# Cluster attention and a softplus layer on one core: the first pass's scores laid upright, a softplus of three operations, loads on SyncE, and the last outputs in other banks

## The chip, the core and the metric

The kernel runs on one core of a Trainium2 chip. TensorE (PE) multiplies matrices into PSUM, VectorE (DVE), ScalarE (ACT) and GpSimd (POOL) work on tiles, and SyncE (SP) issues transfers; DMA engines carry them. The engines run beside each other, each through its own list of instructions in a fixed order, and wait for each other by semaphores. The metric is the time of one execution in microseconds (us) on the device. Before the change the median of three runs is 899.57 us (896.24 to 903.73).

## The reference

```python
# q, k, v: 4 batches x 8 heads x 768 x 64;  centroids: 8 heads x 16 x 64
q_assign = argmax(q_n @ c_n.T); k_assign = argmax(k_n @ c_n.T)   # normed rows, per head
scores = where(q_assign == k_assign, (q @ k.T) / 8, -1e9)
scores -= max(scores);  attn = exp(scores);  attn /= sum(attn) + 1e-9
x = (attn @ v), heads side by side                               # 3072 x 512
h = x @ w_in                                                     # 512 x 2048
g = maximum(h, 0) + log1p(exp(-abs(h)))                          # softplus
out = g @ w_out                                                  # 3072 x 512
```

All inputs are of 32 bits, except the weights, which arrive as 64-bit floats and are converted on the chip. A query attends to the keys of its own cluster alone.

## The kernel before

**Splitting.** Products are made of 16-bit halves: a value is a high half and a low remainder, and three products stand for one. A head's q rows, and its k rows, become two blocks of 128 rows each for the score product: one holds high and low halves of the 64 features, the other the high half again with 16 columns for the cluster (names `n1`, `n2`, turned into `qt` and `kt`). In `kt` the cluster columns hold minus a large number where the key is in another cluster, so the product itself does the masking.

**Tiles and passes.** There are eight passes `pi`, two for each batch, of three blocks of 128 queries; a pass runs over 8 heads, so it has 24 tiles, 192 in all. For a tile, `scores` makes the 128 x 768 product with four matmuls (L576) in a bank pair of the PSUM pool `ps_s` (two of them), DVE takes the row maximum (L592), ACT the exponential (L600). From the second pass on, ACT and POOL split the result in halves (L639, L641) and a DMA transpose, a *flip*, on SP turns two tiles at a time (`pt<-phl`, L226). In the first pass the 32-bit result is turned on PE instead: six transposes (L617) whose results are copied out by ACT (L625) and DVE (L623); the row sums come from the exponential. `attend` multiplies with V: L679 in 32 bits in the first pass, L683 to L685 later. After two heads `attend` divides by the sums (L702, L703, L710: `x`), splits, and flips the result into `xT`.

**The layers.** `ffn1` makes a block of 128 of the 2048 hidden features for 384 queries (L752 to L754), `softplus` has five operations for it (L771, L773, L774, L783 and, for two blocks, L794 and L795), and `ffn2` (L817 to L819) sums eight blocks in the one bank of `ps_o`, which `store` empties on DVE (L833, L837) before the next block of queries may use it. `prep_weights` converts the weights in 32 steps: ACT, DVE three times (L322, L326, L332), ACT, POOL (L336). `prep_k`, `prep_q` and `prep_v` load and lay out the inputs; those of the first pass are turned on PE, the later ones by flips.

**What sets the order.** The whole program is written as generators that yield operations with an engine and a cost in ns. The class `Order` runs them through a small model of the engines and emits each instruction when the model would start it: of all operations that are ready it takes the one that can start first, then the one with the smaller due number. Each engine's list is the result. Where the model sees PE idle for over 600 ns it puts in `int(gap * 0.65 / 52)` small matmuls, *fillers* (L204). Loads of inputs and weights are issued by ACT (L221), flips and stores by SP. A changed cost or operation so moves instructions on every engine.

Of the kernel before, what the change touches and what calls it, by code (L numbers as in the profile page):

```python
# [25 lines left out]
NPE = 8  # L26

# [86 lines left out]
def tile_cluster_attention__then__softplus_ffn(  # L114
# [47 lines left out]
    cf = cpool.tile([P, D], F32, name="cf")  # L162
    nc.sync.dma_start(cf, centroids.rearrange("h c d -> (h c) d"))
    tab = cpool.tile([P, 2 * NT, NCL], F16, name="tab")
# [9 lines left out]
    eye32 = p2.tile([P, P], F32, tag="ot", name="eye32", bufs=QT)  # L174
    nc.gpsimd.tensor_copy(eye32, eye)
# [10 lines left out]
    for i in range(2):  # L186
        t = cpool.tile([P, 2 * NT, P], F16, name=f"n2_{i}")
        nc.gpsimd.memset(t[:, :, D + NCL :], 0.0)
        N2.append(t)


    od = Order()

    eye32_key = od.get("ot", QT)[1]
# [25 lines left out]
    def load(dst, src, nbytes):  # L220
        return op("ACT", 60, lambda: nc.scalar.dma_start(dst, src), dma=nbytes / 290.0)  # L221
# [10 lines left out]
    def prep_centroids():  # L232
        sq = p2.tile([P, D], F32, tag="x32", name="csq", bufs=1)
# [124 lines left out]
    def prep_v(n: int):  # L358

        vk = yield from ring("vb", NP)  # L360
        rk, vf = yield from raw_tile("v", n, [P, 2, NT, D])
        yield load(vf, rows(v, n, 0, NT, 2), P * 2 * NT * D * 4)
        vb = VB[n // 2 % NP]
        raw_v[n] = vf, rk
# [39 lines left out]
    def nearest(xs, heads, low: int, sfx: str, twin: int):  # L404
# [28 lines left out]
        yield op("DVE", 345, lambda: nc.vector.tensor_tensor(sim, sim, tab[:, :nt], ALU.mult))  # L433
# [50 lines left out]
    def clusters(n, ps, eq, hk):  # L484
# [4 lines left out]
        if h % 4 == 0:  # L489
            alive[n] = p2.tile([P, 4, NCL], F16, tag="al", name=f"al_{n}", bufs=4)  # L490
# [8 lines left out]
    def prep_q(n: int, pi: int):  # L499
# [31 lines left out]
        yield op("DVE", 345, lambda: nc.vector.tensor_scalar(n2[:, :, D : D + NCL], sim, MASK, None, ALU.mult))  # L531

# [8 lines left out]
        )  # L541
        aq = p2.tile([P, c12, 1], F16, tag="aq", name=f"aq_{sfx}")
# [16 lines left out]
    pair, sums = {}, {}  # L559

    def scores(t: int):
# [5 lines left out]
        if t:  # L567
            yield wait("sc", t - 1)
# [4 lines left out]
        def emit():  # L573
            for s in range(2):
                for j in range(2):
                    nc.tensor.matmul(  # L576
                        st[:, j, :SH],
                        qt[:, s, i],
                        kt[:, s, NT // 2 * j : NT // 2 * (j + 1)],
# [15 lines left out]
        tot = {}  # L595
        if pi == 0:
            if n // 2 not in sums:
                sums[n // 2] = p2.tile([P, 2 * QT, 1], F32, tag="sum", name=f"sum_{n}", bufs=NP)
            tot["accum_out"] = sums[n // 2][:, n % 2 * QT + i]
        yield op("ACT", 900, lambda: nc.scalar.activation(p32, st[:, :, :SH], AF.Exp, bias=negm, **tot))  # L600
        od.set(sk)
        if pi == 0:

# [23 lines left out]
            if t == H * QT - 1:  # L627
                od.set(eye32_key)
# [286 lines left out]
```

## Time and profile before

| | |
|---|---|
| median of 3 runs | 899.57 us |
| profiled execution, span of its instructions | 899.4 us; no other time is given for it |
| granted clock of PE, mean | 0.992 |
| PE busy | 859.1 us (96%) |
| DVE, ACT, POOL busy | 576.5, 588.2, 528.1 us |
| queue of SP (flips, stores) | 99.15 MB, 56.2% of the DMA engines' span |
| queue of ACT (loads) | 35.66 MB, 13.4% |

A row of the groups reads: line, engine, operation, out<-in by the program's names, shapes and count, then busy us, mean ns of one, and the idle time of the engine just before with what ended it. The chain of waits follows back from the last instruction to what released it. In the table by stages each stretch has the busy time of each engine with its count, PE's granted clock, the mean share of the DMA engines in use and GB/s. Busy times of PE are of matmuls with their latency, so a stream of 512-column matmuls 0.22 us apart shows 0.38 us for each.

### The profile page before, as it was taken

To read this page: it belongs to the slowest core of one execution; us is meant where nothing else is said; L and a number is where in the kernel's file an instruction comes from. 1 tells how busy PE (TensorE), PEld (TensorE's weight loads), DVE (VectorE), ACT (ScalarE), POOL (GpSimd) and SP (SyncE) were. 2 spreads that over 40 slices of the span, in tenths; PEclk is the share of its full clock that TensorE was granted. 3 is DMA by queue.
4 is the path that set the end of the run, shared out by engine and by line. 5 is a ranking of instruction groups with operands and counts; after the bars stand their busy time and mean duration, and the time that the engine had idled before them with its cause. 6 is when DMAs were issued, how large, how long until landed. Compare 5 with 4: busy or idle time off the path is not lost.

```text
span 899.4 us, 20880 instructions
## 1 busy us (share of the span) xinstructions
PE 859.1 (96%) x8650; PEld 562.1 (62%) x8650; DVE 576.5 (64%) x1060; ACT 588.2 (65%) x904; POOL 528.1 (59%) x353
## 2 busy tenths in 40 slices
PE   7889998989889999999999999999999999999997
PEld 7878876655565666655666665555666565655554
DVE  4989997778876656765757666657675655433331
ACT  5667686866757677865858777766787576633330
POOL 5322356787857678866757677675777665512110
PEclk8999999999999999999999999999999999999999
DMA  6323759988896879999696989997888655510000
GB/s 202 117 89 112 154 150 214 202 194 212 168 190 150 189 151 191 226 201 210 149 198 126 187 166 193 195 220 135 182 182 186 145 119 134 111 30 12 25 0 36
DMA packets 393326, 136.12 MB, mean 151 GB/s; under 512 B 369680, under 2 KB 386064, under 8 KB 393232
## 3 DMA queue, kind: packets, MB, share of 16 engines
q1 hardware_dynamic: 371472, 99.15, 56.2%
q10 hardware_dynamic: 21760, 35.66, 13.4%
q8 instruction: 67, 1.10, 0.5%
q14 instruction: 27, 0.22, 0.1%
HBM read 35.68 MB, written 6.29 MB: 47 GB/s over the span
## 4 chain that ended last, share of the span: by engine, by line
PE 73%; DVE 8%; DMA 8%; ACT 4%; issue 3%; POOL 3%; ACTq 1%; POOLq 0%; DVEq 0%
PE s L576 10%; PE o L817 8%; PE o L819 8%; PE o L818 8%; PE h L752 8%; PE h L754 8%; PE h L753 8%; DMA pt<-phl 8%; PE mbank L679 3%; PE mbank L683 3%; PE mbank L685 3%; PE mbank L684 3%; POOL phl L641 2%; PE pT L617 2%; DVE negm L592 2%
## 5 line engine op out<-in xcount | busy, mean ns | idle before, releaser
L641 POOL TENSOR_TENSOR phl<-p,phl 128x768 f16<-128x768 f32 x168 | 278.3, 1672 | 84.8 <-ACT phl L639 61.2
L592 DVE TENSOR_REDUCE negm<-s 128x1 f32<-128x768 f32 x192 | 182.6, 954 | 51.5 <-PE s L576 48.0
L600 ACT ACTIVATE p<-s,negm 128x768 f32<-128x768 f32 x192 | 172.1, 898 | 65.6 <-DVE negm L592 45.5
L795 POOL TENSOR_TENSOR gh<-fg,gh 128x768 f16<-128x768 f32 x64 | 107.2, 1676 | 135.2 <-ACT gh L794 131.8
L752 PE MATMUL h<-xT,wi 128*128 128x384 f16 x512 | 167.4, 327 | 7.4 <-DVE fg L783 5.4
L754 PE MATMUL h<-xT,wi 128*128 128x384 f16 x512 | 167.8, 328 | 0.0
L753 PE MATMUL h<-xT,wi 128*128 128x384 f16 x512 | 167.6, 327 | 0.0
L576 PE MATMUL s<-kt,qt 128*128 128x384 f16 x768 | 155.5, 325 | 3.7 <-ACT p L600 3.3
L819 PE MATMUL o<-wo,gh 128*128 128x512 f16 x384 | 145.8, 380 | 1.1 <-POOL gh L795 1.1
L817 PE MATMUL o<-wo,gh 128*128 128x512 f16 x384 | 146.0, 380 | 0.7 <-DVE ot L837 0.4
L818 PE MATMUL o<-wo,gh 128*128 128x512 f16 x384 | 145.9, 380 | 0.0
L773 ACT ACTIVATE fa<-fa 128x384 f32<-128x384 f32 x128 | 66.6, 521 | 120.1 <-DVE fa L771 119.2
L639 ACT CAST phl<-p 128x768 f16<-128x768 f32 x168 | 134.3, 827 | 16.3 <-DMA pt<-phl 14.1
L771 DVE TENSOR_SCALAR fa<-h 128x384 int32<-128x384 int32 x128 | 71.0, 555 | 107.7 <-PE h L754 107.4
L683 PE MATMUL mbank<-vb,pt 128*128 128x65 f16 x1008 | 108.5, 192 | 8.2 <-DMA pt<-phl 7.8
L684 PE MATMUL mbank<-vb,pt 128*128 128x64 f16 x1008 | 108.5, 192 | 0.0
L685 PE MATMUL mbank<-vb,pt 128*128 128x65 f16 x1008 | 108.2, 194 | 0.0
L683 PEld LDWEIGHTS <-pt 128*128 128x128 f16 x1008 | 93.4, 98 | 22.9 <-DMA pt<-phl 11.4
L783 DVE SCALAR_TENSOR_TENSOR fg<-h,fa 128x384 f32<-128x384 f32 x128 | 70.5, 552 | 53.5 <-ACT fa L774 51.6
L576 PEld LDWEIGHTS <-qt 128*128 128x128 f16 x768 | 71.6, 98 | 49.4 <-issue 6.2
L684 PEld LDWEIGHTS <-pt 128*128 128x128 f16 x1008 | 92.9, 97 | 11.1
L685 PEld LDWEIGHTS <-pt 128*128 128x128 f16 x1008 | 93.1, 97 | 0.0
(122 smaller groups left out, 1289.9 us busy)
## 6 DMA issues: line engine op xcount, KB each, us to landing
wo<-in_moe_w_in_dram ACTq DMA_DIRECT2D x16, 512.0 KB, 3.7
wo<-in_moe_w_out_dram ACTq DMA_DIRECT2D x14, 512.0 KB, 4.0
rawk<-in_k_dram ACTq DMA_DIRECT2D x16, 384.0 KB, 4.7
rawv<-in_v_dram ACTq DMA_DIRECT2D x16, 384.0 KB, 4.6
rawq<-in_q_dram ACTq DMA_DIRECT2D x16, 384.0 KB, 4.1
out_dram<-ot SPq DMA_DIRECT2D x24, 256.0 KB, 2.6
pt<-phl SPq DMA_TRANSPOSE x84, 5.7
wraw<-in_moe_w_out_dram ACTq DMA_DIRECT2D x2, 512.0 KB, 5.3
```

Source lines behind the costliest of these rows:

```text
L576: nc.tensor.matmul(st[:, j, :SH], qt[:, s, i], kt[:, s, NT // 2 * j : NT // 2 * (j + 1)], start=(s == 0), stop=(s == 1),)
L592: yield op("DVE", 950, lambda: nc.vector.tensor_reduce(negm, st[:, :, :SH], AX.XY, ALU.max, negate=True))
L641: "POOL", 1640, lambda: nc.gpsimd.tensor_tensor(phl[:, u, 1], p32, phl[:, u, 0], ALU.subtract), shared=True
L683: nc.tensor.matmul(av, pt[:, 0, c], vb[:, c, D : 2 * D + 1], start=(c == 0), stop=False)
L684: nc.tensor.matmul(av[:, :D], pt[:, 0, c], vb[:, c, :D], start=False, stop=False)
L685: nc.tensor.matmul(av, pt[:, 1, c], vb[:, c, D : 2 * D + 1], start=False, stop=(c == NT - 1))
L752: nc.tensor.matmul(hp, w[0], x[0], start=(c == 0), stop=False)
L753: nc.tensor.matmul(hp, w[0], x[1], start=False, stop=False)
L754: nc.tensor.matmul(hp, w[1], x[0], start=False, stop=(c == NP - 1))
L817: nc.tensor.matmul(po, g[0], wo[:, f, 0, 0], start=(f == f0), stop=False)
L818: nc.tensor.matmul(po, g[0], wo[:, f, 0, 1], start=False, stop=False)
L819: nc.tensor.matmul(po, g[1], wo[:, f, 0, 0], start=False, stop=(f == f0 + NF // 2 - 1))
```

## The change

**First pass.** A new generator `upright` takes the place of scores, exponential and transposes for the 24 tiles of pass 0. It first makes half of the score product (two matmuls, L586: the block with the cluster columns alone), and DVE takes its row maximum (L599). Two small DVE operations (L603, L604) put the negated maximum into two columns of a 128 x 98 tile `mc`, as a multiple of 2048 and a rest; PE turns this (L607) and ACT copies the two rows into rows 96 and 97 of `qt` (L609). The same rows of `kt` hold 2048 and 1. Then the score product is made with keys on the partitions, in twelve matmuls of 128 columns (L619, L620), and the maximum is taken off in the product. ACT's exponential (L638) writes the turned weights at once. The row sums come from a column of ones in V (L730, L752), which is why V of the first heads is laid in rows of 65 and loaded in two parts. Tiles of later passes leave rows 96 and up out of the second block's product.

**Softplus.** exp, ln(1 + .), and then `max(min(a, 20), h)` in place of `|h|`'s sign trick and sum: L771 goes, and the exponential reads PSUM.

**Loads** are issued by SP, and cost the model 450 ns there. **Last outputs:** in the last pass's second half `ffn2` uses the two bank pairs of `ps_s` in place of `ps_o`.

```diff
     def load(dst, src, nbytes):
-        return op("ACT", 60, lambda: nc.scalar.dma_start(dst, src), dma=nbytes / 290.0)
+        return op("SP", 450, lambda: nc.sync.dma_start(dst, src), dma=nbytes / 290.0)
...
+    def upright(t: int):
...
+                nc.tensor.matmul(
+                    st[:, j, :SH], qt[:SHIFT, 1, i], kt[:SHIFT, 1, NT // 2 * j : NT // 2 * (j + 1)],
+                    start=True, stop=True,
+                )
+        yield op("PE", 330, emit)
...
+        yield op("DVE", 950, lambda: nc.vector.tensor_reduce(negm, st[:, :, :SH], AX.XY, ALU.max, negate=True))
+        yield op("DVE", 90, lambda: nc.vector.tensor_scalar(top, negm, 1.0 / by, None, ALU.mult))
+        yield op("DVE", 90, lambda: nc.vector.scalar_tensor_tensor(rest, top, -by, negm, ALU.mult, ALU.add))
...
+        yield op("PE", 60, lambda: nc.tensor.transpose(out=ps[:KROWS], in_=mc, identity=eye))
+        yield op("ACT", 250, lambda: nc.scalar.copy(qt[SHIFT:KROWS, 1, i], ps[SHIFT:KROWS]))
...
+            for c in range(NT):
+                to = up[:, c // (NT // 2), c % (NT // 2) * P : (c % (NT // 2) + 1) * P]
+                nc.tensor.matmul(to, kt[:, 0, c], qt[:, 0, i], start=True, stop=False)
+                nc.tensor.matmul(to, kt[:KROWS, 1, c], qt[:KROWS, 1, i], start=False, stop=True)
+        yield op("PE", 690, emit)
...
+        yield op("ACT", 830, lambda: nc.scalar.activation(dst, up[:, :, :SH], AF.Exp))
...
     def scores(t: int):
...
+        if pi == 0:
+            yield from upright(t)
+            return
...
             for s in range(2):
+                rows = P if s == 0 else SHIFT
                 for j in range(2):
                     nc.tensor.matmul(
                         st[:, j, :SH],
-                        qt[:, s, i],
-                        kt[:, s, NT // 2 * j : NT // 2 * (j + 1)],
+                        qt[:rows, s, i],
+                        kt[:rows, s, NT // 2 * j : NT // 2 * (j + 1)],
...
     def softplus(pi, f, hp, hk):
...
-            lambda: nc.vector.tensor_scalar(a.bitcast(I32), hp.bitcast(I32), -0x80000000, None, ALU.bitwise_or),
-        yield op("ACT", 520, lambda: nc.scalar.activation(a, a, AF.Exp))
+        yield op("ACT", 500, lambda: nc.scalar.activation(a, hp, AF.Exp))
         yield op("ACT", 520, lambda: nc.scalar.activation(a, a, AF.Ln, bias=1.0))
...
-            "DVE", 550, lambda: nc.vector.scalar_tensor_tensor(g[:, f % 2], hp, 0.0, a, ALU.max, ALU.add)
+            "DVE", 550, lambda: nc.vector.scalar_tensor_tensor(g[:, f % 2], a, TOP, hp, ALU.min, ALU.max)
...
     def ffn2(pi: int, half: int, i: int):
...
+        if pi == len(passes) - 1 and half:
+            ok = yield from ring("s", 2)
+            po = ps_s.tile([P, 2, DM], F32, tag="s", name=f"o_{b}_{c0 + i}_{half}")[:, 0]
```

The order on DVE from the first row maximum of the first pass, before (`negm` is the maximum, `ptf` the turned weights of a tile, `wo` and `wi` a weight block under conversion):

```order
L592 TENSOR_REDUCE negm_0_1102<-s_0_1081 128x1
L592 TENSOR_REDUCE negm_1_1107<-s_1_1101 128x1
L332 SCALAR_TENSOR_TENSOR wo<-wo 128x512
L326 SCALAR_TENSOR_TENSOR wo<-wo,wi 128x512
L592 TENSOR_REDUCE negm_2_1143<-s_2_1114 128x1
L623 COPY ptf_0_1115<-pT_0_1_1145 128x384
L592 TENSOR_REDUCE negm_0_1164<-s_0_1148 128x1
L332 SCALAR_TENSOR_TENSOR wo<-wo 128x512
L322 TENSOR_SCALAR wi<-wi 128x512
L623 COPY ptf_0_1115<-pT_1_1_1166 128x384
```

The same engine and place after the change (`mc` is the small tile of the maximum), from the third maximum on:

```order
L599 TENSOR_REDUCE negm_2_1177<-m_2_1136 128x1
L599 TENSOR_REDUCE negm_0_1179<-m_0_1157 128x1
L603 TENSOR_SCALAR mc_118<-negm_2_1177 128x1
L603 TENSOR_SCALAR mc_120<-negm_0_1179 128x1
L604 SCALAR_TENSOR_TENSOR mc_118<-mc_118,negm_2_1177 128x1
L604 SCALAR_TENSOR_TENSOR mc_120<-mc_120,negm_0_1179 128x1
L335 SCALAR_TENSOR_TENSOR wo<-wo,wi 128x512
L599 TENSOR_REDUCE negm_1_1232<-m_1_1181 128x1
L341 SCALAR_TENSOR_TENSOR wo<-wo 128x512
L603 TENSOR_SCALAR mc_118<-negm_1_1232 128x1
L331 TENSOR_SCALAR wi<-wi 128x512
```

The copy of a tile's half is gone and two short operations follow each maximum; weight steps (L331, L335, L341) stand in between more densely: up to the fourth `x` of the program 24 of the 32 blocks are converted, where 18 were.

The order on SP around the first flips of `pt`, before (`xT`, `qt`, `kt`, `pt` are what the flips write):

```order
L226 DMA_TRANSPOSE qt_1_1940<-qn_4_1_1941 128x12x128
L226 DMA_TRANSPOSE pt_4_2031<-phl_3_1980 128x24x128
L226 DMA_TRANSPOSE xT_1420<-xn_0_2056 128x6x128
L226 DMA_TRANSPOSE pt_3_2092<-phl_5_2027 128x24x128
L226 DMA_TRANSPOSE qt_1_1940<-n_1_114 128x12x128
L226 DMA_TRANSPOSE pt_5_2280<-phl_4_2090 128x24x128
```

And after (`wo<-in_moe_w_out` is a weight block's load, `rawq` and `rawk` those of q and k):

```order
L230 DMA wo<-in_moe_w_out_dram 128x512
L230 DMA rawq_2272<-in_q_dram 128x4x192
L235 DMA_TRANSPOSE pt_4_2299<-phl_3_2248 128x24x128
L235 DMA_TRANSPOSE qt_1_2277<-qn_4_1_2278 128x12x128
L235 DMA_TRANSPOSE xT_1524<-xn_0_2313 128x6x128
L230 DMA rawk_2382<-in_k_dram 128x2x384
L235 DMA_TRANSPOSE pt_3_2396<-phl_5_2311 128x24x128
L235 DMA_TRANSPOSE pt_5_2494<-phl_4_2346 128x24x128
L235 DMA_TRANSPOSE kt_2424<-kn_8_2425 128x12x128
L230 DMA wo<-in_moe_w_out_dram 128x512
```

SP's list held flips and stores alone; loads now stand among them, and a load that waits for its buffer stands ahead of flips.

More of the change, by code (lines that the diff above doesn't have):

```diff
@@ L26 @@
 NPE = 8
+TOP = 20.0
+SHIFT = 96
+SHIFT_BY = (2048.0, 1.0)
+KROWS = SHIFT + 2
 REBASE = 2.0**-112
@@ L188, in tile_cluster_attention__then__softplus_ffn @@
         nc.gpsimd.memset(t[:, :, D + NCL :], 0.0)
+        for c, m in zip(range(SHIFT, KROWS), SHIFT_BY):
+            nc.gpsimd.memset(t[:, :, c : c + 1], m)
         N2.append(t)
+    MC = []
+    for i in range(2):
+        t = cpool.tile([P, KROWS], F16, name=f"mc_{i}")
+        nc.gpsimd.memset(t, 0.0)
+        MC.append(t)
     od = Order()
-    eye32_key = od.get("ot", QT)[1]
     mbank = ps_m.tile([P, 512], F32, name="mbank")
@@ L360, in prep_v @@
         vk = yield from ring("vb", NP)
-        rk, vf = yield from raw_tile("v", n, [P, 2, NT, D])
-        yield load(vf, rows(v, n, 0, NT, 2), P * 2 * NT * D * 4)
+        rk, vf1 = yield from raw_tile("v", n, [P, 2, NT, D + (n < H)])
+        vf = vf1[:, :, :, :D]
+        if n < H:
+            yield op("POOL", 150, lambda: nc.gpsimd.memset(vf1[:, :, :, D:], 1.0))
+        parts = 2 if n < H else 1
+        for u in range(0, 2, 2 // parts):
+            yield load(
+                vf[:, u : u + 2 // parts], rows(v, n + u, 0, NT, 2 // parts), P * 2 * NT * D * 4 // parts
+            )
         vb = VB[n // 2 % NP]
-        raw_v[n] = vf, rk
+        raw_v[n] = vf1, rk
         od.set(("vf", n))
@@ L567, in scores @@
         if t:
-            yield wait("sc", t - 1)
+            yield wait("scm" if tiles[t - 1][1] == 0 else "sc", t - 1)
+        if pi == 0:
+            yield from upright(t)
+            return
         sk = yield from ring("s", 2)
@@ L594, in scores @@
         p32 = p2.tile([P, 2, SH], F32, tag="p32", name=f"p32_{sfx}", bufs=3)
[L595 to L600, printed above, removed]
-        od.set(sk)
-        if pi == 0:
-            if u == 0:
-                key = yield from ring("pt", 2)
-                pair[t // 2] = p2.tile([P, 2, NT, P], F32, tag="pt", name=f"ptf_{sfx}"), key
-                od.set(("phl", "new", t))
-            else:
-                yield wait("phl", "new", t - 1)
-            ptf, ptk = pair[t // 2]
-            for j in range(2):
-                hk = yield from ring("h", 2)
-                ps = ps_h.tile([P, NT // 2, P], F32, tag="h", name=f"pT_{sfx}_{j}")
-                def emit(j=j, ps=ps):
-                    for c in range(NT // 2):
-                        nc.tensor.transpose(out=ps[:, c], in_=p32[:, j, c * P : (c + 1) * P], identity=eye32)
-                yield op("PE", 330, emit)
-                dst = ptf[:, u, NT // 2 * j : NT // 2 * (j + 1)]
-                if j:
-                    od.set(pk)
-                    yield op("DVE", 550, lambda: nc.vector.tensor_copy(dst, ps))
-                else:
-                    yield op("ACT", 490, lambda: nc.scalar.copy(dst, ps))
-                od.set(hk)
-            if t == H * QT - 1:
-                od.set(eye32_key)
-            pts[t] = ptf[:, u], ptk
-            od.set(("pt", t))
-            return
+        yield op("ACT", 900, lambda: nc.scalar.activation(p32, st[:, :, :SH], AF.Exp, bias=negm))
+        od.set(sk)
         if u == 0:
```

81 lines of the change are left out of this document (62 added, 19 removed).

## The prediction

> **What bounds the kernel now.** I read the table by stages first, with the borders put at the first score product, the end of the first pass (fourth `x` of L710), the eighth `x`, and the last first-layer matmul. Its columns are the stretch, its length, and the busy time of each engine.
>
> ```profile
> core 0: us, PE busy (x) PEld busy (x) DVE busy (x) ACT busy (x) POOL busy (x), PEclk, DMA share, GB/s
> 0.00:53.10 53.10, 42.73 (x731) 40.70 (x732) 38.48 (x114) 28.73 (x41) 22.75 (x23) 0.94 0.48 156
> 53.10:131.00 77.90, 74.29 (x691) 65.84 (x688) 72.08 (x118) 56.91 (x111) 26.99 (x21) 1.00 0.47 120
> 131.00:245.00 114.00, 100.23 (x1148) 66.97 (x1147) 88.95 (x149) 82.89 (x127) 84.15 (x55) 0.97 0.93 199
> 245.00:300.00 55.00, 50.80 (x585) 34.04 (x583) 38.91 (x71) 37.80 (x56) 34.71 (x24) 1.00 0.85 180
> 300.00:877.30 577.30, 574.07 (x5369) 344.84 (x5366) 334.90 (x606) 379.99 (x569) 357.87 (x231) 1.00 0.72 147
> 877.30:899.40 22.10, 16.95 (x142) 9.69 (x139) 3.19 (x5) 1.88 (x3) 1.64 (x1) 1.00 0.10 36
> ```
>
> From 300 to 877 us PE has work for 574.1 of 577.3 us. Whatever is taken from DVE or ACT there buys at most the 3.2 us left. What can move lies before 300 and in the last 22 us. Part of PE's busy time is filler (L204, matmuls that write nothing anybody reads), as the same table for L204 alone shows; the first number after the length is PE's.
>
> ```profile
> 53.10:131.00 77.90, 7.54 (x126) 7.20 (x126) 1.00 0.47 120
> 131.00:245.00 114.00, 16.18 (x267) 15.12 (x266) 0.97 0.93 199
> ```
>
> So between 131 and 245 us PE has 100.2 − 16.2 = 84.0 us of real work in 114, and no engine is full. Then the chain of waits for these two stages, by line (the views cut these rows off at the right).
>
> ```profile
> by line: PE mbank L679 38.2%; PE pT L617 20.4%; PE s L576 18.4%; PE mbank L204 6.1%; ACT p L600 3.7%; issue 3.5%; DVE negm L592 2.7%; DVE rs L702 2.1%; DVE x L710 1.4%; DVE qn L517 1.2%; DVE ptf L623 0.7%; ACT ptf L625 0.6%; DVE rs L703 0.4
> by line: DMA pt<-phl 10.0%; DVE negm L592 7.4%; PE h L752 7.1%; PE h L754 6.7%; PE h L753 6.6%; issue 5.2%; DVE wo L326 4.7%; PE o L817 4.3%; PE s L576 4.3%; PE o L818 4.1%; PE o L819 4.0%; POOL phl L641 3.9%; PE mbank L683 2.4%; PE mbank L
> ```
>
> In the first pass the chain is PE (77% in three lines), with DVE close behind at 72.1 of 77.9 us busy. In the second stage it changes hands all the time.
>
> **Start (0 to 53).** The loads leave ACT.
>
> ```profile
> 3.75 0.15 DVE L243 TENSOR_SCALAR csg<-css 128x1 f32<-128x1 f32 x1
> ...
> 5.29 1.16 ACTq L221 DMA_DIRECT2D wo<-in_moe_w_in_dram  x1
> 6.50 0.20 ACT L244 ACTIVATE cnrm<-csg 128x1 f32<-128x1 f32 x1 [4.48 <-issue]
> ```
>
> The centroids' logarithm has its input at 3.90 and starts at 6.50, because ACT's sequencer issues loads until 6.45. On SP these stand beside it, and only the centroids' own load goes ahead of the first K load there. All that follows hangs on the centroids, so I take 2.5 us off; the bounds are −4 (later loads come earlier too) and 0 (DVE's work up to 53 us is what counts). The two-part V loads and the small POOL memsets are covered, since nothing reads V before the first scores at 53 us.
>
> **First pass, PE.** Pieces of the chain, with start, length and count:
>
> ```profile
> 38.54 0.37 PE qT L393 x6
> ...
> 58.51 0.65 PE s L576 x4
> 60.44 0.66 PE pT L617 x6
> 65.08 1.29 PE mbank L679 x12
> ```
>
> A tile loses 0.65 + 0.66 = 1.31 us. It gets half a score product (0.33), one small transpose (0.37/6 = 0.06) and twelve 128-column products with their weight loads, for which the six f16 transposes are the nearest row: 2 × 0.37 = 0.74. That is 1.13, or 0.18 less; over 24 tiles **−4.3 us** of PE. The sum column in L730 adds one column to 64: nothing.
>
> **First pass, DVE.** Removed and added, by the rows of the groups (count, busy us, mean ns):
>
> ```profile
> L623 DVE COPY ptf<-pT 128x384 f32<-128x384 f32 x24 | 13.1, 552 | 0.7 <-PE pT L617 0.2
> L702 DVE TENSOR_SCALAR rs<-sum 128x6 f32<-128x6 f32 x4 | 2.4, 602 | 0.0
> L248 DVE SCALAR_TENSOR_TENSOR cnrm<-crn,csg,cnrm 128x1 f32<-128x1 f32 x2 | 1.8, 899 | 0.1
> L249 DVE TENSOR_SCALAR cnrm<-cnrm 128x1 f32<-128x1 f32 x2 | 0.3, 154 | 0.1
> ```
>
> The 24 copies go: −13.1. L752 reads PSUM in place of L702's sums: 2.4 less four at L249's 0.154, so −1.8. For L603 the nearest row is L249: 24 × 0.154 = 3.7. For L604 it is L248, and its two took 0.22 and 1.58 us:
>
> ```profile
> 7.74 1.64 POOL L457 TENSOR_TENSOR kn<-rawk,kn 128x768 f16<-128x768 f32 x1 [5.05 <-ACT kn L455]
> 7.81 1.58 DVE L248 SCALAR_TENSOR_TENSOR cnrm<-crn,csg,cnrm 128x1 f32<-128x1 f32 x1
> ```
>
> The long one ran beside a POOL operation and ended with it. POOL is busy 27.0 of 77.9 us in this stage; with that chance (0.35) of meeting an operation, and half of one to wait (a weight operation of POOL takes 17.11/14 = 1.2 us, next table), L604 costs 0.22 + 0.21, or 10.3 for 24. The ends are 5.3 (none waits) and 37.9 (all do). Sum of the small edits: −13.1 − 1.8 + 3.7 + 10.3 = −0.9, so nothing is won here. The Trainium skill's page "SBUF — State Buffer", section "SBUF: two separate sides", says that a VectorE operation with two SBUF inputs and a GpSimd operation that reads SBUF exclude each other for the whole instruction; L604 is such an operation. By that rule no wait is shared out, and the bad end of 37.9 is reached if POOL always comes first; the pair of rows above agrees.
>
> What DVE does besides matters more. The order shows that up to the fourth `x` it has converted 24 weight blocks (18 before), and up to the first row maximum 5 (4 before). So this stage takes five blocks more, and the next five fewer. Weight work alone, in the table by stages: the second busy time is DVE's, the last POOL's, with one operation for each block (14 and 11).
>
> ```profile
> 53.10:131.00 77.90, 0.00 (x0) 23.38 (x31) 18.00 (x27) 17.11 (x14) 1.00 0.47 120
> 131.00:245.00 114.00, 21.17 (x84) 28.29 (x31) 13.23 (x20) 12.83 (x11) 0.97 0.93 199
> ```
>
> A block costs DVE 23.38/14 = 1.67 us here and 28.29/11 = 2.57 later. DVE's sum is 72.1 − 0.9 + 5 × 1.67 = 79.6 us. At its present filling (72.1/77.9) the stage takes 86.0, **+8.1**; if PE keeps setting the pace, −4.3. Neither row is nearer, so I take the middle, **+2**. ACT loses 24 copies and gains 24 short ones and has 21 us free. PE, DVE and ACT hand a tile on more often now, and its two score products each hold a bank until a reader is done:
>
> ```profile
> L592 DVE TENSOR_REDUCE negm<-s 128x1 f32<-128x768 f32 x192 | 182.6, 954 | 51.5 <-PE s L576 48.0
> L600 ACT ACTIVATE p<-s,negm 128x768 f32<-128x768 f32 x192 | 172.1, 898 | 65.6 <-DVE negm L592 45.5
> ```
>
> That is 0.33 + 0.95 and 0.74 + 0.90 us, 2.9 in all, or 1.5 for each of the two banks, below the 77.9/24 = 3.2 us that a tile takes; so the longer way of a tile is covered by its neighbours.
>
> **Filling stage (131 to 245).** DVE loses five blocks, 5 × 2.57 = 12.9, and one operation of each softplus:
>
> ```profile
> L771 DVE TENSOR_SCALAR fa<-h 128x384 int32<-128x384 int32 x16 | 8.8, 553 | 11.3 <-PE h L754 11.2
> ```
>
> Together 21.7 of its 89.0 us. ACT is rid of its load issues, POOL of five weight operations. The full 21.7 returns if DVE's turns in the chain are what holds the others up; nothing returns if DMA does (share 0.93). DVE holds 7.4% and 4.7% in two lines, DMA 10.0%; I take half, **−11**. After 245 the relief meets a PE at 50.8 of 55, and after 300 a full one: nothing. The order has 31 fillers less than before, 31 × 7.54/126 = 1.9 us of PE, all where PE waits anyway: nothing.
>
> **Tail.**
>
> ```profile
> 877.51 0.56 DVE L771 TENSOR_SCALAR fa<-h 128x384 int32<-128x384 int32 x1 [2.21 <-PE h L754]
> 878.10 0.52 ACT L773 ACTIVATE fa<-fa 128x384 f32<-128x384 f32 x1 [3.46 <-DVE fa L771]
> 882.48 0.39 PE L819 MATMUL o<-wo,gh 128*128 128x512 f16 x1 [1.11 <-POOL gh L795]
> ...
> 882.92 0.38 PE L818 MATMUL o<-wo,gh 128*128 128x512 f16 x1
> 883.14 0.38 PE L819 MATMUL o<-wo,gh 128*128 128x512 f16 x1
> 883.56 0.69 DVE L837 SCALAR_TENSOR_TENSOR ot<-o,ot 128x512 f32<-128x512 f32 x1 [3.79 <-PE o L819]
> 884.30 0.38 PE L817 MATMUL o<-wo,gh 128*128 128x512 f16 x1 [0.20 <-DVE ot L837]
> ```
>
> The last softplus gets from h to ACT 0.59 us sooner, and PE waits for its end at 882.48. Back to back these matmuls start 0.22 us apart, so the bank's drain costs 884.30 − 883.36 = 0.94 us, twice: with scores' banks both go. 0.59 + 1.88 = **−2.5**.
>
> **Sum.** The profiled execution's span is 899.4, 0.2 below the median of the runs shown: 899.4 − 2.5 + 2 − 11 − 2.5 = **885.4**, say 885.5.
>
> **Unpriced: rows of 96 and 98.** No row shows a matmul with fewer than 128 rows.
>
> ```profile
> L576 PEld LDWEIGHTS <-qt 128*128 128x128 f16 x768 | 71.6, 98 | 49.4 <-issue 6.2
> L679 PEld LDWEIGHTS mbank<-rawv,ptf 128*128 128x128 f32 x288 | 34.5, 192 | 0.7
> ```
>
> At 98 ns the load hides under a 0.65/4 = 162 ns product; at the slowest row, 192, each of the 336 shortened products of later passes would show 30 ns, 10 us. I take nothing, as the nearer row is L576.
>
> **Rivals.** *All of DVE's relief arrives*: the first pass keeps PE's pace and the filling stage gives back 21.7: 899.4 − 2.5 − 4.3 − 21.7 − 2.5 = 868.4. For it speaks that no engine's own work is above 0.78 of that stage; against, that every weight block still has to be loaded.
>
> *The filling stage is DMA's*: it returns nothing, and 899.4 − 2.5 + 2 − 2.5 = 896.4 remains, with 892 to 903 around it. For it speaks the share of 0.93: the change moves the transfers to another queue and makes none smaller.
>
> *Slower: SP's queue.* In the order 43 loads stand among the flips after the first `pt` flip, 20 of 84 `pt` flips have one right ahead, and eleven of these loads wait for POOL or ACT to free a buffer. Such a wait holds every flip behind it.
>
> ```profile
> SPq L226 <- POOL phl L641: 123.4, 40, 7.5
> ...
> DMA to landing us min/median/max: 3.2/4.1/9.7
> ```
>
> A wait of SP for POOL lasts 123.4/40 = 3.1 us. Eleven of them, all reaching PE, make 34: 919. The point is (908.6 − 885.5)/3.1 = 7.5 of them. Against it: PE stands still for only 3.2 us in 577 now, so flips have room. The Trainium skill's page "DMA: Bandwidth & Descriptors", section "Queues, rings and completion order", says that a DMA engine takes turns between queues but works through one queue in order. By that rule a load that shares SP's queue, 4.1 us from issue to landing on its own, would also have to outlast the flip in front of it; no row of this case shows a load on SP among flips.
>
> **Chances.** Forecast 0.45, its own range 880 to 892 (the filling stage returns a quarter to three quarters); all relief 0.16; DMA's stage 0.26; SP's queue 0.13. A measurement here tells 1% from no change: 890.6 and 908.6 are the marks. Faster: 0.40 of the forecast's 0.45, and the 0.16, make 0.56. Same: 0.05 + 0.26 = 0.31. Slower: 0.13. The range 868 to 904 leaves out SP's queue and the thin ends of the others.
>
> **What would show it.** The centroids' logarithm near 4 us and the first score product near 50.5. L599 to L604 without 1.6 us operations, or with them. The fourth `x` near 130; if it comes at 124 or 137, the middle was wrong. The eighth `x` at 11 us less after the fourth than the present 114: at the same distance, DMA holds that stage. Between that and the last h PE at 99%; gaps before L734 behind `pt` flips mean SP's queue. No wait for L886 in the last 15 us. A PEld row far above 98 ns for `qt` would make the unpriced term real.

## The result and the profile after

The changed kernel takes 877.05 us in the median of four runs (875.09 to 877.72), beside 900.79 for the kernel before on the same chip (896.24 to 903.73): a ratio of 0.9749, with a 95% interval of 0.9702 to 0.9795. That is 8.5 us below the forecast of 885.5: inside the whole range of 868 to 904, but below the 880 to 892 that the forecast gave as its own. The profiled execution has a span of 873.3 us, 26.1 less than the 899.4 of before.

The table by stages of the changed kernel, with the same borders as in the prediction (first score product, about the fourth and the eighth `x`, last first-layer matmul) and one more at 250. Columns: stretch, length, busy time of each engine, PE's granted clock, DMA share, GB/s.

```profile
core 0: us, PE busy (x) PEld busy (x) DVE busy (x) ACT busy (x) POOL busy (x), PEclk, DMA share, GB/s
0.00:49.70 49.70, 39.73 (x740) 37.78 (x741) 38.67 (x114) 29.62 (x44) 24.27 (x32) 1.00 0.68 209
49.70:130.80 81.10, 75.72 (x901) 68.94 (x899) 72.78 (x156) 53.98 (x95) 31.52 (x26) 1.00 0.41 112
130.80:227.00 96.20, 91.58 (x1061) 62.03 (x1060) 66.97 (x117) 71.57 (x111) 74.84 (x50) 0.98 1.11 218
227.00:250.00 23.00, 22.20 (x258) 15.56 (x257) 18.83 (x31) 17.60 (x26) 15.30 (x11) 1.00 0.82 154
250.00:300.00 50.00, 50.00 (x534) 31.49 (x533) 29.48 (x52) 39.72 (x59) 39.16 (x26) 1.00 1.05 190
300.00:853.60 553.60, 552.76 (x5147) 331.53 (x5145) 274.80 (x485) 361.87 (x548) 339.89 (x220) 1.00 0.80 148
853.60:873.30 19.70, 14.93 (x111) 8.05 (x109) 2.63 (x4) 1.85 (x3) 1.64 (x1) 0.96 0.11 41
```

The same table for the fillers alone (L213 after the change; PE's busy time stands behind the length):

```profile
49.70:130.80 81.10, 13.67 (x219) 12.71 (x220) 1.00 0.41 112
130.80:227.00 96.20, 13.07 (x195) 11.89 (x193) 0.98 1.11 218
227.00:250.00 23.00, 6.53 (x112) 6.16 (x112) 1.00 0.82 154
250.00:300.00 50.00, 0.00 (x0) 0.00 (x0) 1.00 1.05 190
```

And one row that the prediction did not look at, the fillers (L204) of the kernel *before* between 245 and 300 us:

```profile
245.00:300.00 55.00, 8.50 (x147) 7.90 (x144) 1.00 0.85 180
```

Take the fillers off PE's busy time and what is left of each stretch is time in which PE had no work. Before: 114 − 84.0 = 30.0 us in the filling stage, 55 − 42.3 = 12.7 from 245 to 300, about 4 in the long stretch. After: 96.2 − 78.5 = 17.7, then 23 − 15.7 = 7.3, nothing from 250 to 300, 1.6 in the long stretch. PE is full from about 250 us on, not from 300.

| border | before | after | stage changed by |
|---|---|---|---|
| first score product | 53.1 | 49.7 | −3.4 |
| fourth `x` | 130.3 | 130.1 | +3.2 |
| eighth `x` | 243.1 | 226.1 | −16.8 |
| last first-layer matmul | 877.1 | 853.4 | −6.7 |
| end | 899.4 | 873.3 | −2.4 |

Each column is one profiled execution. Three later kernels that run the same order through these stages (less to load, one bank for the last outputs, the other form of L604) have the first score product at 49.9 to 50.9, the first pass at 80.3 to 81.9 and the filling stage at 95.3 to 97.2. So a difference of less than 2 us in a stage is no finding.

At the borders of this table the −16.8 of the filling stage is 10.8 us of PE's time without work (28.7 to 17.9) and 5.9 us of work (84.0 to 78.1). Behind it PE's time without work falls by 9.4 us (18.7 to 9.3), and its work grows by 2.7: part of the work has only moved into the next stage. So the two stages are best taken together: −23.5.

The chain of waits of the two middle stages (49.7 to 130.8 and 130.8 to 227), by line:

```profile
by line: PE mbank L730 28.1%; DVE negm L599 13.5%; PE u L619 7.0%; PE u L620 6.1%; issue 5.2%; PE m L586 4.1%; ACT ptf L638 4.1%; DVE mc L604 3.9%; DVE wo L341 3.1%; DVE wo L335 2.4%; PE mbank L213 2.1%; ACT p L681 2.1%; DVE wo L331 2.1%; P
by line: PE h L802 10.4%; PE h L804 9.8%; PE h L803 9.8%; PE s L662 9.2%; PE mbank L213 6.5%; PE o L868 5.5%; DMA rawk<-in_k_dram 5.4%; PE o L866 5.4%; PE o L867 5.4%; PE mbank L736 4.4%; PE mbank L734 4.3%; PE mbank L735 4.2%; DVE negm L67
```

In the first pass PE's share in the products and transposes of a tile fell from 77% to 45% (L730, L619, L620, L586), and DVE's maximum with what follows it came up. In the filling stage the flips (`pt<-phl`, 10.0% before) are gone from the head of the chain, and so are DVE's weight steps; PE's own lines lead, with one load of K (`rawk`, 5.4%) among them.

How long PE's weight loads waited for flips, before and after (us in total, times, longest):

```profile
PEld L683 <- DMA pt<-phl: 11.4, 9, 3.7
```

```profile
PEld L734 <- DMA pt<-phl: 1.2, 4, 0.6
```

The rival "SP's queue" did not come. Weight loads do wait on SP for POOL to free a buffer, 17 times:

```profile
SPq L230 <- POOL wi L345: 56.1, 12, 9.2
...
SPq L230 <- POOL wo L345: 17.5, 5, 4.9
```

But all 17 waits lie ahead of the first `pt` flip, which goes out at 130.4; the loads of the first layer's weights (`wo<-in_moe_w_in`) go out between 7.6 and 65.7 us. From 130.4 on, where the rival had eleven waits of 3.1 us, loads wait for POOL three times, 4.0 us in all:

```profile
SPq L230 <- POOL vb L388: 2.5, 1, 2.5
SPq L230 <- POOL kn L473: 1.5, 2, 1.2
```

### The profile page after: what moved, and what is told of

Its sections match the earlier page's. It is cut to its first block, busy times and chain, and to the rows that moved or that the text cites. A ratio compares the mean times of both kernels' runs of the same rounds, so it can differ in the third digit from the quotient of the medians.

```text
span 873.3 us, 20893 instructions
## 1 busy us (share of the span) xinstructions
PE 846.9 (97%) x8739; PEld 555.4 (64%) x8739; DVE 504.2 (58%) x956; ACT 576.2 (66%) x880; POOL 526.6 (60%) x362
## 3 DMA queue, kind: packets, MB, share of 16 engines
q8 instruction: 68, 1.11, 0.5%
## 4 chain that ended last, share of the span: by engine, by line
PE 73%; issue 10%; DVE 7%; POOL 3%; ACT 2%; DMA 2%; SPq 2%; POOLq 0%; DVEq 0%; ACTq 0%
PE s L662 11%; PE h L802 8%; PE h L804 8%; PE h L803 8%; PE o L866 7%; PE o L868 7%; PE o L867 7%; PE mbank L736 3%; PE mbank L734 3%; PE mbank L735 3%; PE mbank L730 3%; POOL gh L840 2%; SPq L230 2%; PE mbank L213 1%; DVE negm L599 1%
## 5 line engine op out<-in xcount | busy, mean ns | idle before, releaser
L678 DVE TENSOR_REDUCE negm<-s 128x1 f32<-128x768 f32 x168 | 160.2, 955 | 113.4 <-PE s L662 112.7
L681 ACT ACTIVATE p<-s,negm 128x768 f32<-128x768 f32 x168 | 150.9, 900 | 54.5 <-DVE negm L678 36.3
L818 ACT ACTIVATE fa<-h 128x384 f32<-128x384 f32 x128 | 62.4, 489 | 125.9 <-PE h L804 125.4
L662 PE MATMUL s<-kt,qt 128*128 128x384 f16 (+1 forms) x672 | 136.6, 325 | 3.4 <-ACT p L681 3.2
L828 DVE SCALAR_TENSOR_TENSOR fg<-fa,h 128x384 f32<-128x384 f32 x128 | 70.5, 550 | 115.2 <-ACT fa L819 112.9
L662 PEld LDWEIGHTS <-qt 128*128 128x128 f16 (+1 forms) x672 | 62.0, 98 | 43.9 <-issue 4.9
L803 PEld LDWEIGHTS <-wi 128*128 128x128 f16 x512 | 49.8, 97 | 34.2 <-issue 2.5
```

The lines of the kernel that those rows point to most:

```text
L662: nc.tensor.matmul(st[:, j, :SH], qt[:rows, s, i], kt[:rows, s, NT // 2 * j : NT // 2 * (j + 1)], start=(s == 0), stop=(s == 1),)
L678: yield op("DVE", 950, lambda: nc.vector.tensor_reduce(negm, st[:, :, :SH], AX.XY, ALU.max, negate=True))
L803: nc.tensor.matmul(hp, w[0], x[1], start=False, stop=False)
```

## The experiments

The forecast summed four terms, so the first question is whether the parts add up at all. Ratios are to the kernel before, with their 95% intervals; the full change is 0.9749 (0.9702 to 0.9795).

### One part alone

**Loads on SP, nothing else.**

```diff
 # the kernel before
-        return op("ACT", 60, lambda: nc.scalar.dma_start(dst, src), dma=nbytes / 290.0)
+        return op("SP", 450, lambda: nc.sync.dma_start(dst, src), dma=nbytes / 290.0)
```

> The kernel before with one part of the change: loads issued from SyncE instead of ScalarE (and the planner's cost for them). My theory (VectorE's relief made the gain): only the start gains, 2.5 to 3.4 us, the filling stage keeps its length of 113 us, so about 897. Rival one (ScalarE's queue: loads that sit in it hold its own work, and on SP they go out earlier): most of the gain is here, 12 to 20 us, 880 to 888, with the last weight block converted some 30 us sooner than 274.6. Rival two (SP's queue holds the flips): over 905.

890.51 us, ratio 0.9892 (0.9852 to 0.9931). Between the two theories. The start did not gain: the first score product came at 56.0, 2.9 us later than before, though the centroids' logarithm ran at 3.3. In the new plan seven weight blocks had reached GpSimd's step by then, where before it was four. The filling stage went from 112.8 to 93.5 us (by the `x` of the fourth and eighth group), and no wait for a flip is left among those of PE.

**The short softplus, nothing else** (L771 removed, the exponential reading PSUM, minimum and maximum last).

> The kernel before with one part of the change: the softplus without its VectorE operation (exp, log, and a minimum and maximum). My theory: half of 16 x 0.55 us in the filling stage and 0.6 us in the tail, so about 5 us less, 895. All of VectorE's relief arriving: 9.4 us less, 890. If the filling stage is not VectorE's: 0.6 us less, 899.

898.81 us, ratio 0.9994 (0.9968 to 1.002): no change that can be measured. Yet in its trace the filling stage is 10.4 us shorter (102.4 after 112.8), and the stretch from there to the last first-layer matmul 7.4 us longer. So the relief arrives in its stage and most of it is lost behind it; why, no run shows. PE's waits for `pt` flips, 7.0 us after 11.4, have not taken it.

**The upright first pass, nothing else** (with all that belongs to it; loads, softplus and outputs as before).

> The kernel before with one part of the change: the first pass with upright scores (and the shorter rows in the later score products, the small table and the storage that belong to it); loads, softplus and outputs as before. My theory: first pass 2 to 3 us longer, filling stage half of 12.9 us shorter because five weight blocks are done earlier, so about 4 us less, 896. If the order of the weight blocks was moved by the loads and not by the first pass: 2 to 3 us more, 902 to 903. If the upright pass is what bought the whole gain: 885 or less.

920.99 us, ratio 1.0228 (1.0178 to 1.0278): slower by 21 us, and all three expectations missed. The pass itself, from the first score product to the fourth `x`, took 78.7 us, 1.5 more than before. The loss is elsewhere: the first score product came at 60.0 (53.1 before), GpSimd's step for the last weight block began at 309.4 (277.5), and PE's weight loads waited twice as long for flips:

```profile
PEld L734 <- DMA pt<-phl: 23.9, 25, 5.1
```

In the chain of its filling stage (138.6 to 251.4) the flips come first by far, 42.1% where it was 10.0%:

```profile
by line: DMA pt<-phl 42.1%; issue 10.0%; POOL phl L692 4.4%; DVE negm L678 4.1%; DVE wo L341 3.2%; DVE fg L833 3.1%; DVE wo L335 2.9%; ACT fa L823 2.5%; ACT p L681 2.4%; ACT phl L690 2.3%; PE h L802 1.9%; ACT fa L824 1.7%; PE mbank L734 1.7
```

### One part taken away

**The changed kernel with its loads back on ScalarE,** planned and issued as before.

```diff
 # the changed kernel
-        return op("SP", 450, lambda: nc.sync.dma_start(dst, src), dma=nbytes / 290.0)
+        return op("ACT", 60, lambda: nc.scalar.dma_start(dst, src), dma=nbytes / 290.0)
```

> The changed kernel with its loads back on ScalarE (cost 60 as before). The upright pass issues V in halves, so ScalarE issues three more loads before the centroids' logarithm. Theory one (the upright pass needs the loads on SP: the start comes 7 us late and the planner converts the weights later): 20 to 30 us more than the changed kernel, 897 to 907. Theory two (the four parts add up): the 9.6 us that the loads alone bought come back, 887. Theory three (my forecast's terms): 2.5 us more, 879.5.

915.72 us, ratio 1.0202 (1.0166 to 1.0238): 39 us above the changed kernel, more than any theory said. So the load line, for which the forecast had 2.5 us, decides whether the rest is a gain or a loss. The start shows part of the reason. In order of time: start, length, what; in the last bracket the idle time before it.

```profile
3.47 0.64 ACTq L230 DMA_DIRECT2D wo<-in_moe_w_in_dram  x1
...
4.15 5.11 ACTq L230 DMA_DIRECT2D rawv<-in_v_dram  x3
9.30 0.20 ACT L253 ACTIVATE cnrm<-csg 128x1 f32<-128x1 f32 x1 [7.29 <-issue]
```

The upright pass loads V in halves, so ScalarE has three more transfers to issue ahead of the logarithm, 5.11 us for the three. The logarithm ran at 9.30, and the first score product came at 60.0.

**The longer softplus back.**

> The changed kernel with the longer softplus (VectorE's sign operation back). Theory one (VectorE is not what holds the filling stage once the loads are on SP): 0.6 us in the tail and little more, 877 to 880. Theory two (my forecast: VectorE's relief counts by half): 5 us more, 882. Theory three (VectorE's relief counts in full): 9.4 us more, 886.5.

891.66 us, ratio 0.9919 (0.9899 to 0.9939): 14.6 us above the changed kernel, more than the 9.4 us of the theory that counts the softplus in full. What was worth nothing on the kernel before is worth 1.7% here.

**The upright pass taken away** (loads, softplus and banks of the change on the kernel before).

> The kernel before with all parts but the upright pass: loads on SP, short softplus, scores' banks for the last outputs. If the parts add up: 890.5 - 1.3 - 1.9 = 887, and the upright pass, which alone cost 21 us, would bring 10 us here. If the upright pass costs by itself wherever it stands: below 870. If loads and softplus overlap in what they relieve: 888 to 890.

879.74 us, ratio 0.979 (0.976 to 0.982). None of the expected numbers. The upright pass, the largest edit by far, is worth 2.7 us here by the medians, and since the intervals overlap it may be worth nothing. The trace shows two shifts of opposite sign: without it the first pass is shorter (75.6 us against 80.4) and the start longer (56.3 against 49.7).

**The last outputs back in one bank.**

> The changed kernel with its last outputs back in the one bank: my theory says that the two drains of 0.94 us between the last three outputs return, so 1.9 us more than the changed kernel (about 879), and everything before the last 22 us is unchanged. Rival: the outputs' banks hold the scores of the last tiles too, and the change of banks costs or buys something before the tail.

878.96 us, ratio 0.9772 (0.9733 to 0.981): 1.9 us, as forecast, though too little to be told from no change by the times. The trace shows it, with PE waiting for the drain:

```profile
863.00 0.69 DVE L882 SCALAR_TENSOR_TENSOR ot<-o,ot 128x512 f32<-128x512 f32 x1 [3.77 <-PE o L864]
863.74 0.38 PE L862 MATMUL o<-wo,gh 128*128 128x512 f16 x1 [0.20 <-DVE ot L882]
```

In the changed kernel the only wait of PE in the last 20 us is for POOL:

```profile
PE o L868 <- POOL gh L840: 1.0, 1, 1.0
```

So the parts don't add: alone, the three that were run apart make −1.1%, −0.1% and +2.3%; together with the banks they make −2.5%. By stages, in the same way as in the table of borders (us; "behind it" is from the eighth `x` to the last first-layer matmul; "all but upright" has the loads, the softplus and the banks):

| kernel | to the first score product | first pass | filling stage | behind it | tail |
|---|---|---|---|---|---|
| before | 53.1 | 77.2 | 112.8 | 634.1 | 22.3 |
| loads alone | 56.0 | 75.7 | 93.5 | 641.6 | 22.3 |
| softplus alone | 51.8 | 77.2 | 102.4 | 641.5 | 21.9 |
| upright alone | 60.0 | 78.7 | 112.8 | 644.7 | 22.8 |
| all but upright | 56.3 | 75.6 | 91.0 | 638.0 | 19.7 |
| all | 49.7 | 80.4 | 96.0 | 627.3 | 19.9 |

The loads alone, with the sign operation still on VectorE, shorten the filling stage by more than the whole change does, and 7.5 us of it return behind it. For the filling stage and what is behind it together, the loads alone make −11.8, the short softplus alone −3.0, the upright pass alone +10.6; all but the upright pass make −17.9, and everything −23.5.

### Is it the queue or the plan?

The load line does two things: it sends a transfer through another queue, and it tells the planner another cost, which moves instructions on every engine. Two kernels take these apart.

**The plan of the changed kernel, kept word for word on every engine; loads issued by ScalarE.**

```diff
 # the changed kernel
-        return op("SP", 450, lambda: nc.sync.dma_start(dst, src), dma=nbytes / 290.0)
+        return op("SP", 450, lambda: nc.scalar.dma_start(dst, src), dma=nbytes / 290.0)
```

> The changed kernel with every engine's order kept word for word, but the loads issued from ScalarE at their place in that order. (The run with the loads back and planned as before took 915.7; this keeps the plan.) Theory one (it is the queue: loads on ScalarE hold its own work at the start and share the DMA engines with the flips from a second queue): 905 to 916. Theory two (it is the order that the planner makes when a load costs SP 450 ns and ScalarE nothing: weights earlier, first pass earlier): 880 to 885, of which about 4 at the start because ScalarE issues loads ahead of the centroids' logarithm.

883.48 us, ratio 0.9792 (0.977 to 0.9814; the kernel before took 902.47 beside it). Theory two. The centroids' logarithm runs at 6.21 instead of 3.32, and the first score product comes at 52.3 instead of 49.7, the 2.6 us that the forecast's first term asked for. PE's waits for flips are back in part:

```profile
PEld L734 <- DMA pt<-phl: 6.4, 7, 1.8
```

Since the order is the same, the flips can be compared one to one. From 131 to 300 us, issue to landing in the median, changed kernel first, then this one:

```profile
pt<-phl SPq DMA_TRANSPOSE x22, 6.6
xT<-xn SPq DMA_TRANSPOSE x7, 3.3
```

```profile
pt<-phl SPq DMA_TRANSPOSE x22, 7.7
xT<-xn SPq DMA_TRANSPOSE x7, 5.0
```

With the loads in a second queue a flip lands 1.1 to 1.7 us later in the median. The `pt` flips can be parted by whether a load is on its way at the same time: with none they take 5.9 and 5.7 us in the two kernels (8 and 7 flips), with one 6.9 and 8.1 (14 and 15). So beside a load a flip takes about 1.0 us longer in one queue with it, and 2.4 in another. The Trainium skill's page "DMA: Bandwidth & Descriptors", section "Queues, rings and completion order", says that a DMA engine takes turns between the queues that have work, a packet at a time; these rows agree with it, though they show landings and not turns. The prediction had used only the other half of the rule, that flips would wait behind loads in one queue, and not that two queues share.

**The plan made for ScalarE, but loads issued by SP.**

```diff
 # the changed kernel
-        return op("SP", 450, lambda: nc.sync.dma_start(dst, src), dma=nbytes / 290.0)
+        return op("ACT", 60, lambda: nc.sync.dma_start(dst, src), dma=nbytes / 290.0)
```

> The changed kernel planned as if its loads cost ScalarE 60 ns (the plan of the run that took 915.7), but issued from SyncE at their place in that order. Theory one (the plan makes nearly all of it): 905 to 912, some 5 us below 915.7, as the queue alone was worth with the other plan, most of it at the start. Theory two (plan and queue are only bad together): 880 to 890. If loads on SP among flips in an order made without regard to SP hold the flips: above 916, with longer waits of PE for the flips of pt.

890.38 us, ratio 0.9897 (0.987 to 0.9924). Theory one falls, and theory two's range of 880 to 890 is missed by 0.4. The four cells, as ratios to the kernel before:

| | loads issued by SP | loads issued by ScalarE |
|---|---|---|
| planned for SP (450 ns) | 0.9749 | 0.9792 |
| planned for ScalarE (60 ns) | 0.9897 | 1.0202 |

The plan is worth 1.5% with SP's queue and 4.1% with ScalarE's; the queue 0.4% with the one plan and 3.1% with the other. The 0.4% is not clear of noise, as the two intervals (0.9702 to 0.9795 and 0.977 to 0.9814) overlap. With the plan for ScalarE, moving the loads to SP takes the first score product from 60.0 to 52.0 and shortens PE's waits for flips, from the first row (loads on ScalarE) to the second (loads on SP):

```profile
PEld L734 <- DMA pt<-phl: 17.1, 13, 5.1
```

```profile
PEld L734 <- DMA pt<-phl: 4.5, 6, 1.5
```

From the end of the first pass to 300 us the `pt` flips land 0.7 us sooner with the loads on SP (7.0 after 7.7 in the median), the six or seven `xT` flips no sooner (4.4 after 4.1).

What stands out between the two plans is when weight blocks are converted; that this alone makes the difference is not shown. With the plan for SP, GpSimd's step, the last of a block, has begun for 23 of the 32 blocks by the fourth `x`, and for the last at 242.6 us; with the other plan, on the same queue, for 20 and at 295.9. The first pass is 3.1 us shorter with the later blocks (77.3 against 80.4), and more than that is lost after it.

### Is it VectorE or the DMA engines?

**VectorE's sign operation back, order kept.** 128 operations of 0.55 us stand on VectorE ahead of the exponentials, with the old last operation; the order of everything else is kept.

```diff
 # the changed kernel
-        yield op("ACT", 500, lambda: nc.scalar.activation(a, hp, AF.Exp))
+        yield op("ACT", 500, lambda: (
+            nc.vector.tensor_scalar(a.bitcast(I32), hp.bitcast(I32), -0x80000000, None, ALU.bitwise_or),
+            nc.scalar.activation(a, a, AF.Exp)))
```

> The changed kernel with every engine's order kept, with VectorE's sign operation put back ahead of each exponential (128 x 0.55 us of VectorE) and the old last operation of the softplus. (Planned anew, the longer softplus took 891.7.) Theory one (VectorE's time and the longer way of a softplus are what the filling stage and PE's waits hang on): 888 to 893, the filling stage 4 to 9 us longer and waits of PE after 300 us. Theory two (it is the plan: the order made for the shorter softplus is the better one): 877 to 880. In both 0.6 us of it is the tail.

895.55 us, ratio 0.9924 (0.9901 to 0.9947): 1.75% above the changed kernel, as much as when it was planned anew (0.9919). The time is above theory one's 888 to 893, on a chip where the kernel before took 902.47, and far from theory two. So it is VectorE's time and the longer way of a softplus, which this run does not tell apart, and not the order. The rows of its filling stage and the long stretch, and PE's longest waits:

```profile
131.40:233.40 102.00, 91.50 (x1061) 60.52 (x1060) 78.73 (x134) 71.80 (x111) 74.53 (x50) 1.00 1.05 206
...
300.00:872.60 572.60, 565.50 (x5265) 338.38 (x5264) 331.56 (x595) 372.71 (x561) 347.18 (x225) 1.00 0.79 146
```

```profile
PE s L662 <- ACT p L681: 8.4, 13, 1.7
PE h L802 <- DVE fg L828: 5.1, 8, 1.1
```

The filling stage is 6.0 us longer for the 16 sign operations in it, 8.8 us of VectorE: two thirds of VectorE's time arrives. After 300 us PE is busy 565.5 of 572.6 where the changed kernel has 552.8 of 553.6: 6.3 us more that it stands still in the stretch for which the forecast had "nothing".

**Less to load, order kept.**

```diff
 # the changed kernel
-        yield load(kf, rows(k, n, 0, NT, 2), P * 2 * NT * D * 4)
+        yield load(kf if n < H else kf[:, :, :2], rows(k, n, 0, NT if n < H else 2, 2), P * 2 * NT * D * 4)
```

V is cut in the same way, both for all later batches, Q to a third after the first pass, and two fixed buffers take the place of the rotating ones, with the planner's cost unchanged. The edit leaves two of six blocks of K and V, a third and not the sixth that the expectation names: in the filling stage nine loads shrink from 384 to 128 KB, 2.4 MB less.

> The changed kernel with the order kept and less to load: of K and V of the second batch only a sixth is read, of Q after the first pass only a third; the rest of each buffer holds older values, so the output is not the reference's, but every other operation stands. In the filling stage that takes some 9 loads of 384 KB to 64 or 128 KB, 2.9 MB less; at that stage's 217 GB/s, 13 us, if the DMA engines set its pace. Theory one (DMA sets the pace of the filling stage): it gets 8 to 13 us shorter, about 866. Theory two (VectorE and the hand-overs set it): at most 2 us, 875 to 877.

874.93 us, ratio 0.9698 (0.9671 to 0.9724), overlapping the changed kernel's. The filling stage, with its DMA share of 1.07 and 196 GB/s:

```profile
131.80:227.10 95.30, 90.17 (x1060) 60.36 (x1059) 67.06 (x117) 72.15 (x111) 74.62 (x50) 1.00 1.07 196
```

It is 95.3 us long against 96.0. A share of 1.1 looked like a stage held by the DMA engines; a tenth of the bytes less moved it by 0.7 us. Theory two: the loads' bytes don't set the pace. The test is narrower than it looks, because most of the packets' time is the flips', which it leaves as they are. The kernel before, where the two have queues of their own, shows it from 131 to 245 us (packets, MB, share; flips and stores, then loads):

```profile
q1 hardware_dynamic: 58801, 14.84, 67.7%
q10 hardware_dynamic: 4112, 7.73, 24.9%
```

If the packets' time set the pace, the share of 1.07 after 1.11 would have made 4%, some 4 us; that was not seen either. Whether fewer flips would shorten the stage was not tried.

### One disputed cost by itself

**L604 with one tile input**, the maximum as the operation's second scalar.

```diff
 # the changed kernel
-nc.vector.scalar_tensor_tensor(rest, top, -by, negm, ALU.mult, ALU.add)
+nc.vector.tensor_scalar(rest, top, -by, negm, ALU.mult, ALU.add)
```

> The changed kernel with L604 in another form: the same value from one tile input, with the negated maximum as the operation's second scalar, in place of an operation with two tile inputs. By the reading that an operation of VectorE with two SBUF inputs waits beside one of GpSimd: no L604 above 0.2 us (now up to 0.93), 24 x (0.304 - 0.16) = 3.5 us less of VectorE in the first pass, at most 3 us off the time. If the waits come from GpSimd in whatever form: durations up to 0.9 us remain and the time is the same.

877.0 us, ratio 0.9754 (0.9728 to 0.9781): the same time. But the operation itself did what was expected. Changed kernel, then this one (shortest, median and longest in ns):

```profile
L604 DVE SCALAR_TENSOR_TENSOR mc<-mc,negm x24: 151/163/933, 52.3 to 122.1; 128x1 f16<-128x1 f16 x24
```

```profile
L604 DVE TENSOR_SCALAR mc<-mc,negm x24: 204/216/218, 53.5 to 123.2; 128x1 f16<-128x1 f16 x24
```

In the changed kernel seven of the 24 took more than 0.2 us: each began while GpSimd was at work and ended some 20 ns after GpSimd's operation. In the other form ten began beside GpSimd, and none took more than 218 ns. So the waits beside GpSimd are gone, and 7.2 us became 4.9, though the operation itself is dearer (216 after 163 ns in the median). The Trainium skill's page "SBUF — State Buffer", section "SBUF: two separate sides", names two SBUF inputs as one of the conditions for such a wait, and the pair agrees. The first pass took 80.3 us after 80.4: that 2.3 us less of VectorE bring nothing speaks against VectorE's sum as what sets that stage's length.

No kernel beat the changed one by more than the measurement can tell.

## Why the prediction was right, and where it was not

The forecast was faster by 14 us for the profiled execution; it was 26.1. The direction was right. The filling stage and the stretch behind it gave 23.5 us where the forecast had 11, so the place was right and its size was not; and the load line, which had no price there, has a large part in it.

**Start, −2.5: right** (−3.4), and for its reason: with the order kept, ScalarE's queue costs 2.6 us there. The logarithm ran here:

```profile
3.32 0.20 ACT L253 ACTIVATE cnrm<-csg 128x1 f32<-128x1 f32 x1 [1.31 <-DVE csg L252]
```

But the plan can undo it: with loads on SP and nothing else the start was 2.9 us longer.

**First pass, +2: right** (+3.2), though by a choice between two ends neither of which happened. I had PE's pace at −4.3 and a full VectorE at +8.1. PE's real work fell as counted (62.0 us after 66.8), while PE stood without work for 19 us; VectorE came to 72.8 us rather than 79.6 and was no fuller than before. By the chain above what set the length was the way of a tile from PE to VectorE, back to PE, to ScalarE and to PE again; no run tests that by itself. The sentence "the longer way of a tile is covered by its neighbours" failed. That +2 came near +3.2 is luck: it was the middle of two values for which no row spoke more.

**L604, 0.43 us each, 10.3 us: too much.** It measured 0.304:

```profile
L604 DVE SCALAR_TENSOR_TENSOR mc<-mc,negm 128x1 f16<-128x1 f16 x24 | 7.2, 304 | 0.4
```

The share that met an operation of GpSimd was as forecast, 8 of 24, and they waited some 0.4 us each rather than 0.6; the operation by itself took 0.16 us rather than 0.22. Neither bad end was near, and the run with the other form shows that the time did not hang on it.

**Filling stage, −11 as half of VectorE's relief, and nothing behind it: the terms that were mis-sized.** They measured −16.8 and −6.7. The half was chosen because the DMA share was 0.93, and that share does not hold the stage: packets that take as long in sum (0.93 × 114 = 106 us before, 1.11 × 96.2 = 107 after) fit into 18 us less. And VectorE was taken for the only source. The loads alone make −11.8 in the two stages, with the sign operation in place; the forecast had put their effect there at nothing, and with it the flips, for which PE waited 11.4 us before and 1.2 after. How much of the 23.5 is VectorE's stays open: in the changed kernel its sign operation is worth two thirds of its time in the filling stage, and on the kernel before it was worth nothing in the end. That PE's time without work in the filling stage fell by 10.8 us, almost the 11 of the forecast, is therefore no proof of the half.

**"After 245 the relief meets a PE at 50.8 of 55, and after 300 a full one: nothing": wrong up to 300.** The 50.8 holds 8.5 us of fillers, as the row above shows; PE had 12.7 us to spare there, and 7.3 after the change, from 227 to 300. I took fillers off in the two stages before and not in this one. After 300 PE had about 4 us without work and gave back 2.5. And "full" there is no fixed state: with the sign operation put into the changed kernel's order PE has 7.8 us without work in that stretch.

**Tail, −2.5: right** (−2.4), 1.9 of it the banks.

**Rows of 96 and 98: nothing, right.** Blocks of 96, 128 and 98 rows load alike:

```profile
L662 PEld LDWEIGHTS <-qt 96*128 96x128 f16 x336 | 32.9, 98 | 21.9
L662 PEld LDWEIGHTS <-qt 128*128 128x128 f16 x336 | 29.1, 98 | 22.0 <-issue 4.9
L620 PEld LDWEIGHTS <-kt 98*128 98x128 f16 x144 | 14.1, 98 | 1.7 <-issue 1.4
```

**The rivals.** *All of the relief arrives* gave 868.4 and was as near in the time (8.7 us off by the medians) as the forecast (8.5), with the filling stage closer to it and the first pass not. *DMA's stage* is refuted for the loads by the run with less to load, and as "returns nothing" by the stage itself, which moved 199 GB/s before and 218 after. *SP's queue* is refuted in the changed kernel, and the flips were held more with the loads on the other queue. What no rival named was that the other three edits without the load line make the kernel 2% slower, and that with it the upright pass, the largest of them, adds nothing that can be measured.

## What to carry to other kernels

Where a planner sets the order, a line that changes a cost is not priced by the operations that it adds or removes: keep the plan and move the queue, and move the plan and keep the queue, before crediting either. Take fillers off in every stage alike, and call a stage DMA-bound only when taking transfers away shortens it. A part that gains nothing alone may be worth most in company, so time parts by taking them away from the whole as well as by adding them one at a time.

## What the hardware showed that was not expected

In the kernel with the upright pass alone a load takes ScalarE 0.33 to 0.40 us to issue, in the median of each group. But at the start, where many are issued in a row, single ones took up to 3.0 us, and in the changed kernel with its loads back three took 5.11:

```profile
L230 ACTq DMA_DIRECT2D rawv<-in_v_dram x20: 374/396/2999, 2.8 to 648.6; - x20
```

SyncE takes longer, 0.55 us in the median of the changed kernel's 85 loads and up to 3.5 us, but there no computation stands behind it. And a DMA share near or over 1 (the times of all packets are summed) went with a stage whose length did not depend on the loads' bytes: 218 GB/s became 196, and the stage kept its length within 0.7 us.
